# Sliding-window attention with sinks, then an MLP: one phase of matmul 1 and one mixed phase per batch, fp32 loads cast on the chip

## The chip, the cores and the metric

The kernel runs on one core of one Trainium2 chip. The time is the device time of one execution in microseconds (us). The kernel before takes 262.4 us (median of two executions, 262.15 to 262.66).

Engines: PE (TensorE, matmuls), PEld (its weight loads), DVE (VectorE), ACT (ScalarE), POOL (GpSimd), SP (the sync engine, which here only issues transfers).

## The reference

```python
# q, k, v: (4 batches, 8 heads, 768 tokens, 64); n_sink = 4, window = 128; all fp32
scores = (1 / sqrt(64)) * q @ k.T                      # per batch and head
keep = (key < n_sink) | ((0 <= query - key) & (query - key < window))
a = softmax(where(keep, scores, -1e9))
x = (a @ v), heads side by side                        # (3072 tokens, 512)
h = x @ w_in                                           # (512 -> 2048)   "matmul 1"
g = h * sigmoid(1.702 * h)
out = g @ w_out                                        # (2048 -> 512)   "matmul 2"
```

## The kernel before

A "unit" is a pair of heads of one batch (16 units). A loop over the units does attention for unit s, the AV product of unit s - 1, and, as filling between them, eight groups of matmul 1 and one or two tiles of matmul 2 of what is ready. All loads of q, k, v and the weights go through GpSimd's queue, which casts fp32 to fp16 on the way (by the page of this kernel 27.79 MB were read, and this queue, q0, wrote 13.64 MB). PSUM is the memory of the tiles that this kernel's matmuls write; DVE's copies below (0.41 to 0.42 us) take the transposes out of it.

```python
for hl in range(2):                        # loads of a unit: one head of q or k at a time, cast by the queue
    nc.gpsimd.dma_start(qn[:, :, hl], q[b, h0 + hl].rearrange("(i s) d -> s i d", s=P))
    nc.gpsimd.dma_start(kn[:, :, hl], k[b, h0 + hl].rearrange("(i s) d -> s i d", s=P))
...
for j in range(3):                         # t_chunk: transposes of q and k on PE, copied out of PSUM by DVE
    tp = misc_bank(f"tqk{su}_{j}", (P, 2, 2, P), FP16)
    ...
    nc.vector.tensor_copy(out=qkT[:, :, 2 * j * P : (2 * j + 2) * P], in_=tp)   # contiguous rows
...
for s in range(NU):                        # one unit of attention, matmul 1 and matmul 2 between its parts
    ...
    if s < 3:
        load_w_in(s + 1)
    elif s < 7:
        load_w_out(s - 3)
    fs = claim_f(s, 8)                     # matmul 1 groups that are ready
    m2 = claim_mm2(s, 2)                   # matmul 2 tiles that are ready
    s_chunk(s, 0); t_chunk(s + 1); av_chunk(s - 1, 0); s_chunk(s, 1); av_chunk(s - 1, 1)   # abridged
    ...                                    # f_chunk and mm2_chunk among xt_chunk(s - 1, ...)
    mask_chunk(s)
```

The softmax here doesn't subtract the row's maximum and nothing guards it: scores larger than these inputs give would overflow.

Of the kernel before, what the change touches and what calls it, by code (L numbers as in the profile page):

```python
# [9 lines left out]
FP32 = mybir.dt.float32  # L11
FP16 = mybir.dt.float16
AF = mybir.ActivationFunctionType
ALU = mybir.AluOpType
# [3 lines left out]
ACOLS = 1920  # L18
NQB = 6


def _acol(J: int, q0: int) -> int:
    if J == 0:
        return q0
    if J == 5:
        return 768 + (q0 - 640)
    return 896 + 256 * (J - 1) + (q0 - 128 * J)


def _build_mask(n_sink: int, window: int) -> np.ndarray:  # L30
    mask = np.zeros((P, ACOLS), dtype=np.float32)
    jj = np.arange(P)
    for J in range(6):
        if J == 0:
            qr = np.arange(0, 768)
        elif J == 5:
            qr = np.arange(640, 768)
        else:
            qr = np.arange(128 * J, 128 * J + 256)
        cols = np.array([_acol(J, int(t)) for t in qr])  # L40
        key = 128 * J + jj
        rel = qr[None, :] - key[:, None]
        keep = (key[:, None] < n_sink) | ((rel >= 0) & (rel < window))
        mask[:, cols] = keep.astype(np.float32)
    return mask.astype(np.float16)


SCORE_TILES = [
    ("s0", [(0, 0, 512)], 0),
    ("s1", [(0, 512, 256), (5, 640, 128)], _acol(0, 512)),  # L50
    ("s2", [(1, 128, 256), (2, 256, 256)], _acol(1, 128)),
    ("s3", [(3, 384, 256), (4, 512, 256)], _acol(3, 384)),
]
# [3 lines left out]
def kernel(  # L57
# [13 lines left out]
    assert (H, Dh) == (8, 64) and S == 768  # L71
# [6 lines left out]
    NU = Bsz * NHP  # L78
    NF = d_ff // P
    TT = 384  # L80
    NT4 = TT // P
# [3 lines left out]
    mask_d = nc.inline_tensor(_build_mask(n_sink, window), name="cmask")  # L85
# [3 lines left out]
    xtp = ctx.enter_context(tc.tile_pool(name="xtp", bufs=1))  # L89
    attn = ctx.enter_context(tc.tile_pool(name="attn", bufs=2))  # L90
    moep = ctx.enter_context(tc.tile_pool(name="moep", bufs=2))
    psp = ctx.enter_context(tc.tile_pool(name="psum", bufs=1, space=bass.MemoryType.PSUM))

    ident16 = const.tile([P, P], FP16, name="ident16")
    nc.sync.dma_start(ident16, ident16_d.ap())
    mask_all = const.tile([P, ACOLS], FP16, name="maskall")
    nc.sync.dma_start(mask_all, mask_d.ap())
    w_in16 = wpool.tile([P, 4, d_ff], FP16, name="w_in16")
    w_out16 = wpool.tile([P, NF, d_model], FP16, name="w_out16")
    xT = [xtp.tile([P, Bsz * S], FP16, name=f"xT{i}") for i in range(NHP)]  # L100

    def load_w_in(i: int):
        nc.gpsimd.dma_start(w_in16[:, i], moe_w_in[bass.ts(i, P), :])
# [7 lines left out]
    def sc_bank(name, shape=(P, 512), dt=FP32):  # L111
        return psp.tile(list(shape), dt, tag="sc", bufs=4, name=name)

    def ht_bank(name):
        return psp.tile([P, TT], FP32, tag="hT", bufs=2, name=name)

    def misc_bank(name, shape, dt):
        return psp.tile(list(shape), dt, tag="misc", bufs=2, name=name)

    U = [dict() for _ in range(NU)]  # L120

    def loads_qk(u: int):
        b, hp = divmod(u, NHP)
        h0 = 2 * hp
        su = f"{b}_{hp}"
        qn = attn.tile([P, NQB, 2, D], FP16, tag="qn", bufs=3, name=f"qn{su}")
        kn = attn.tile([P, NQB, 2, D], FP16, tag="kn", bufs=3, name=f"kn{su}")
        for hl in range(2):
            nc.gpsimd.dma_start(
                qn[:, :, hl], q[b, h0 + hl].rearrange("(i s) d -> s i d", s=P)  # L130
            )
            nc.gpsimd.dma_start(
                kn[:, :, hl], k[b, h0 + hl].rearrange("(i s) d -> s i d", s=P)
            )
        U[u].update(qn=qn, kn=kn)

    def loads_v(u: int):
        b, hp = divmod(u, NHP)
        h0 = 2 * hp
        su = f"{b}_{hp}"  # L140
        v65 = attn.tile([P, 2, NQB, D + 1], FP16, tag="v65", bufs=4, name=f"v65{su}")
        nc.vector.memset(v65, 1.0)
        nc.gpsimd.dma_start(  # L143
            v65[:, :, :, 0:D], v[b, h0 : h0 + 2].rearrange("h (i s) d -> s h i d", s=P)
        )
        U[u]["v65"] = v65

    def t_chunk(u: int):
        su = f"u{u}"
        qn, kn = U[u]["qn"], U[u]["kn"]  # L150
        qkT = attn.tile([P, 2, S], FP16, tag="qkT", bufs=2, name=f"qkT{su}")
        for j in range(3):
            tp = misc_bank(f"tqk{su}_{j}", (P, 2, 2, P), FP16)
            for i in range(2):
                I = 2 * j + i
                nc.tensor.transpose(tp[:, 0, i], qn[:, I], ident16)  # L156
                nc.tensor.transpose(tp[:, 1, i], kn[:, I], ident16)
            nc.vector.tensor_copy(out=qkT[:, :, 2 * j * P : (2 * j + 2) * P], in_=tp)
        U[u]["qkT"] = qkT

    def s_chunk(u: int, part: int):
        su = f"u{u}"
        qkT = U[u]["qkT"]
        if part == 0:
            U[u]["AT"] = attn.tile([P, 2, ACOLS], FP16, tag="AT", name=f"AT{su}")
        AT = U[u]["AT"]
        qT = [qkT[bass.ts(hl, D), 0] for hl in range(2)]
        kT = [qkT[bass.ts(hl, D), 1] for hl in range(2)]
        for nm, mms, c0 in SCORE_TILES[2 * part : 2 * part + 2]:
            st = [sc_bank(f"{nm}{su}_{hl}") for hl in range(2)]  # L170
            col = 0
            for J, q0, w in mms:
                for hl in range(2):
                    nc.tensor.matmul(  # L174
                        st[hl][:, col : col + w],
                        kT[hl][:, bass.ts(J, P)],
                        qT[hl][:, q0 : q0 + w],
                        start=True,
                        stop=True,
                    )  # L180
                col += w
            for hl in range(2):
                nc.scalar.activation(  # L183
                    out=AT[:, hl, c0 : c0 + col], in_=st[hl][:, 0:col],
                    func=AF.Exp, scale=scale,
                )

    def mask_chunk(u: int):
        AT = U[u]["AT"]
        for hl in range(2):  # L190
            nc.vector.tensor_tensor(
                out=AT[:, hl], in0=AT[:, hl], in1=mask_all, op=ALU.mult
            )

    def av_chunk(u: int, g: int):
        su = f"u{u}"
        AT, v65 = U[u]["AT"], U[u]["v65"]
        av = misc_bank(f"av{su}_{g}", (P, 3, 2, D + 1), FP32)
        xnat = attn.tile([P, 3, 2, D], FP16, tag="xnat", bufs=2, name=f"xn{su}_{g}")
        rcp = attn.tile([P, 3, 2], FP32, tag="rcp", bufs=2, name=f"rcp{su}_{g}")  # L200
        for i3 in range(3):
            I = 3 * g + i3
            Js = [J for J in (I - 1, I) if J >= 0] + ([0] if I >= 2 else [])
            for hl in range(2):
                for n, J in enumerate(Js):
                    c = _acol(J, P * I)
                    nc.tensor.matmul(
                        av[:, i3, hl],
                        AT[:, hl, c : c + P],
                        v65[:, hl, J],  # L210
                        start=(n == 0),
                        stop=(n == len(Js) - 1),
                    )
        nc.vector.reciprocal(out=rcp, in_=av[:, :, :, D])
        nc.vector.tensor_tensor(
            out=xnat, in0=av[:, :, :, 0:D],
            in1=rcp.to_broadcast((P, 3, 2, D)), op=ALU.mult,
        )
        U[u][f"xn{g}"] = xnat

    def xt_chunk(u: int, g: int):
        b, hp = divmod(u, NHP)
        su = f"u{u}"
        xnat = U[u][f"xn{g}"]
        xt = misc_bank(f"xt{su}_{g}", (P, 3, P), FP16)
        for i3 in range(3):
            nc.tensor.transpose(xt[:, i3], xnat[:, i3], ident16)
        c0 = b * S + 3 * g * P
        nc.vector.tensor_copy(out=xT[hp][:, c0 : c0 + 3 * P], in_=xt)

    gT = {}
    for bb in range(Bsz):
        for j in range(2):
            gT[bb, j] = moep.tile([P, NF, TT], FP16, tag="gT", name=f"gT{bb}_{j}")

    def f_chunk(b: int, j: int, F: int, nth: int):
        tok0 = b * S + j * TT
        su = f"{b}_{j}_{F}"
        hT = sc_bank(f"hT{su}", (P, TT)) if nth < 2 else ht_bank(f"hT{su}")
        for c in range(4):  # L240
            nc.tensor.matmul(  # L241
                hT, w_in16[:, c, bass.ts(F, P)], xT[c][:, tok0 : tok0 + TT],
                start=(c == 0), stop=(c == 3),
            )
        th = moep.tile([P, TT], FP16, tag="th", bufs=3, name=f"th{su}")
# [27 lines left out]
    def claim_f(s: int, cap: int):  # L273
        got = []
        while len(got) < cap and f_fifo and f_ready[f_fifo[0][0]] <= s:
# [4 lines left out]
            if f_done[bj] == NF:  # L280
                mm2_ready[bj] = s + 1
# [105 lines left out]
```

## Time and profile before

| stretch | PE busy | what holds |
|---|---|---|
| 0 to 50 us | 33.1 of 50 us | loads: the queues' share is at nine tenths |
| 50 to 256 us | 204.9 of 206 us | the matmul stream itself |

From the page of the kernel before: the span, and three rows of it in 40 equal slices of 6.5 us. A digit is the busy share of the slice in tenths; the last row is what the queues moved in GB/s.

```profile
span 260.1 us, 4792 instructions
PE   0749787999999999999999999999999999999993
DMA  9999999999959393595960140101021011111112
GB/s 137 139 175 182 176 173 175 179 174 136 92 73 117 20 115 20 106 63 73 61 79 35 8 65 22 59 3 40 4 79 44 0 42 40 43 40 40 40 43 81
```

The stretches of the same trace: start and end, length, then busy time of each engine (with instructions), the granted clock of PE, the queues' share (the times of all packets added up, so it can exceed 1; it is not the digit of the DMA row) and GB/s.

```profile
core 0: us, PE busy (x) PEld busy (x) DVE busy (x) ACT busy (x) POOL busy (x), PEclk, DMA share, GB/s
0.00:25.00 25.00, 13.08 (x107) 7.56 (x108) 11.62 (x21) 10.51 (x21) 20.91 (x30) 1.00 1.67 155
25.00:50.00 25.00, 20.04 (x265) 12.44 (x263) 22.98 (x51) 16.82 (x37) 19.70 (x25) 1.00 1.93 176
50.00:256.00 206.00, 204.90 (x1521) 111.43 (x1520) 123.95 (x250) 110.40 (x225) 33.70 (x40) 1.00 0.49 59
```

The period of the steady regime is read from ACT's line of time: start, duration, instruction. The same exp comes back two units later.

```profile
107.40 0.59 ACT L183 ACTIVATE ATu_1622<-s0u_0_1623 128x512 f16<-128x512 f32 x1
136.65 0.59 ACT L183 ACTIVATE ATu_2032<-s0u_0_2033 128x512 f16<-128x512 f32 x1
```

So a batch (four units) takes 2 x 29.25 = 58.5 us. Of that, 32 groups of matmul 1 take 0.65 us each (20.8 us) and six tiles of matmul 2 take 3.45 us each (20.7 us); the rest, 17 us, is attention, 4.25 us of PE time per unit.

### The profile page before, as it was taken

To read this page: it belongs to the slowest core of one execution; us is meant where nothing else is said; L and a number is where in the kernel's file an instruction comes from. 1 tells how busy PE (TensorE), PEld (TensorE's weight loads), DVE (VectorE), ACT (ScalarE), POOL (GpSimd) and SP (SyncE) were. 2 spreads that over 40 slices of the span, in tenths; PEclk is the share of its full clock that TensorE was granted. 3 is DMA by queue.
4 is the path that set the end of the run, shared out by engine and by line. 5 is a ranking of instruction groups with operands and counts; after the bars stand their busy time and mean duration, and the time that the engine had idled before them with its cause. 6 is when DMAs were issued, how large, how long until landed. Compare 5 with 4: busy or idle time off the path is not lost.

```text
span 260.1 us, 4792 instructions
## 1 busy us (share of the span) xinstructions
PE 238.2 (92%) x1888; PEld 131.4 (51%) x1888; DVE 158.6 (61%) x320; ACT 138.4 (53%) x282; POOL 74.3 (29%) x92
## 2 busy tenths in 40 slices
PE   0749787999999999999999999999999999999993
PEld 0415444565646464555546464555545555555541
DVE  4337989898958685495918684493915833543300
ACT  1257666868438483757538483757533633644311
POOL 8977788773535151133310100000000000000000
PEclk9999999999999999999999999999999999999999
DMA  9999999999959393595960140101021011111112
GB/s 137 139 175 182 176 173 175 179 174 136 92 73 117 20 115 20 106 63 73 61 79 35 8 65 22 59 3 40 4 79 44 0 42 40 43 40 40 40 43 81
DMA packets 81607, 20.76 MB, mean 80 GB/s; under 512 B 75697, under 2 KB 78001, under 8 KB 81585
## 3 DMA queue, kind: packets, MB, share of 16 engines
q0 software_dynamic: 77696, 13.64, 66.1%
q1 hardware_dynamic: 3888, 6.82, 7.1%
q8 instruction: 15, 0.25, 0.4%
q14 instruction: 8, 0.06, 0.1%
HBM read 27.79 MB, written 6.29 MB: 131 GB/s over the span
## 4 chain that ended last, share of the span: by engine, by line
PE 82%; ACT 5%; DVE 4%; POOL 3%; DMA 3%; issue 1%; ACTq 0%; POOLq 0%
DMA qn_2_126<-in_q_dram 3%; PE o_1_2_3359 L257 1%; PE o_1_1_3339 L257 1%; PE o_1_0_3319 L257 1%; PE o_0_2_3267 L257 1%; PE o_0_1_3215 L257 1%; PE o_0_0_3163 L257 1%; PE o_1_2_3079 L257 1%; PE o_1_1_3027 L257 1%; PE o_1_0_2975 L257 1%; PE o_0_2_2809 L257 1%; PE o_0_1_2771 L257 1%; PE o_1_2_2584 L257 1%; PE o_1_1_2395 L257 1%; PE o_0_1_1985 L257 1%; PE o_0_0_1965 L257 1%
## 5 line engine op out<-in xcount | busy, mean ns | idle before, releaser
L241 PEld LDWEIGHTS <-w_in_77 128*128 128x128 f16 x512 | 47.8, 98 | 31.4 <-issue 1.1
L257 PEld LDWEIGHTS <-gT_1_90 128*128 128x128 f16 x48 | 4.7, 98 | 5.5
L257 PEld LDWEIGHTS <-gT_0_89 128*128 128x128 f16 x48 | 4.7, 98 | 5.3
L257 PEld LDWEIGHTS <-gT_0_87 128*128 128x128 f16 x48 | 4.7, 98 | 5.3
L257 PEld LDWEIGHTS <-gT_1_88 128*128 128x128 f16 x48 | 4.7, 98 | 5.3
L257 PEld LDWEIGHTS <-gT_1_84 128*128 128x128 f16 x48 | 4.7, 98 | 5.2
L257 PEld LDWEIGHTS <-gT_0_85 128*128 128x128 f16 x48 | 4.7, 98 | 5.2
L257 PEld LDWEIGHTS <-gT_1_86 128*128 128x128 f16 x48 | 4.7, 98 | 5.2
L156 PE MATMUL tqku_0_108<-ident_73,qn_0_91 128*128 128x128 f16 x2 | 0.6, 288 | 7.1 <-DMA qn_0_91<-in_q_dram 7.1
L257 PEld LDWEIGHTS <-gT_0_83 128*128 128x128 f16 x48 | 4.7, 98 | 4.8
L143 POOL DMA_DIRECT2D v_3_2433<-in_v_dram x1 | 1.0, 1007 | 15.3 <-issue 15.3
L183 ACT ACTIVATE ATu_136<-s0u_0_137 128x512 f16<-128x512 f32 x1 | 0.6, 597 | 7.9 <-PE s0u_1_138 L174 7.9
L156 PEld LDWEIGHTS <-qn_0_91 128*128 128x128 f16 x6 | 0.7, 125 | 7.1 <-issue 7.1
L247 DVE SCALAR_TENSOR_TENSOR gT_0_87<-th_0_6_2420,hT_0_6_2415 128x384 f16<-128x384 f16 x1 | 0.6, 553 | 5.9 <-ACT th_0_6_2420 L246 5.9
L257 PE MATMUL o_0_0_1145<-w_out_78,gT_0_83 128*128 128x512 f16 x16 | 4.1, 379 | 0.0
L247 DVE SCALAR_TENSOR_TENSOR gT_1_88<-th_1_6_2796,hT_1_6_2791 128x384 f16<-128x384 f16 x1 | 0.6, 554 | 5.7 <-ACT th_1_6_2796 L246 5.7
L247 DVE SCALAR_TENSOR_TENSOR gT_0_85<-th_0_6_1600,hT_0_6_1595 128x384 f16<-128x384 f16 x1 | 0.6, 553 | 5.3 <-ACT th_0_6_1600 L246 5.3
L247 DVE SCALAR_TENSOR_TENSOR gT_1_86<-th_1_6_2010,hT_1_6_2005 128x384 f16<-128x384 f16 x1 | 0.6, 553 | 5.3 <-ACT th_1_6_2010 L246 5.3
L257 PE MATMUL o_0_2_1360<-w_out_78,gT_0_83 128*128 128x512 f16 x16 | 3.8, 379 | 0.0
L257 PE MATMUL o_0_0_1965<-w_out_78,gT_0_85 128*128 128x512 f16 x16 | 3.8, 379 | 0.0
L257 PE MATMUL o_1_2_2584<-w_out_78,gT_1_86 128*128 128x512 f16 x16 | 3.8, 379 | 0.0
L257 PE MATMUL o_1_0_2375<-w_out_78,gT_1_86 128*128 128x512 f16 x16 | 3.8, 379 | 0.0
(1546 smaller groups left out, 810.9 us busy)
## 6 DMA issues: line engine op xcount, KB each, us to landing
w_in_77<-in_moe_w_in_dram POOLq DMA_DIRECT2D x4, 512.0 KB, 8.6
w_out_78<-in_moe_w_out_dram POOLq DMA_DIRECT2D x4, 512.0 KB, 8.8
maskall<-cmask SPq DMA_DIRECT2D x1, 480.0 KB, 3.9
out_dram<-osb_0_0_1146 SPq DMA_DIRECT2D x1, 256.0 KB, 2.1
out_dram<-osb_0_1_1166 SPq DMA_DIRECT2D x1, 256.0 KB, 3.6
out_dram<-osb_0_2_1361 SPq DMA_DIRECT2D x1, 256.0 KB, 3.6
out_dram<-osb_1_0_1556 SPq DMA_DIRECT2D x1, 256.0 KB, 3.7
out_dram<-osb_1_1_1576 SPq DMA_DIRECT2D x1, 256.0 KB, 2.3
```

The source lines that it names most:

```text
L143: nc.gpsimd.dma_start(v65[:, :, :, 0:D], v[b, h0 : h0 + 2].rearrange("h (i s) d -> s h i d", s=P))
L156: nc.tensor.transpose(tp[:, 0, i], qn[:, I], ident16)
L183: nc.scalar.activation(out=AT[:, hl, c0 : c0 + col], in_=st[hl][:, 0:col], func=AF.Exp, scale=scale,)
L241: nc.tensor.matmul(hT, w_in16[:, c, bass.ts(F, P)], xT[c][:, tok0 : tok0 + TT], start=(c == 0), stop=(c == 3),)
L247: nc.vector.scalar_tensor_tensor(out=gT[b, j][:, F], in0=th, scalar=1.0, in1=hT, op0=ALU.add, op1=ALU.mult)
L257: nc.tensor.matmul(ops, gT[b, j][:, F, bass.ts(t4, P)], w_out16[:, F], start=(F == 0), stop=(F == NF - 1),)
```

## The change

Its intent: fewer, larger instructions and a simpler stream for PE. Per batch there is a phase of matmul 1 alone, then a phase in which matmul 2 is mixed with the attention of the next batch. Attention goes by half-units (one pair of heads, 384 of the 768 tokens). q, k and v are loaded as fp32 by the sync queue, q and k with three successive tokens on one partition (768 bytes in a piece), and cast on DVE, GpSimd and ACT. The weights wait behind batch 0's loads, and batch 1's loads behind the weights. Part of the mask becomes GpSimd selects.

The diff, cut to its core (the matmul code, the mask and the pools are left out; cuts are marked):

```diff
-            nc.gpsimd.dma_start(
-                qn[:, :, hl], q[b, h0 + hl].rearrange("(i s) d -> s i d", s=P)
-            )
+            nc.sync.dma_start(                                   # loads(m): two units, 384 tokens, fp32
+                qk32[:, t].rearrange("p h i d -> p h (i d)"),
+                s[b, hs, t0 : t0 + SLAB].rearrange("h (p i) d -> p h (i d)", i=NB),
+            )
+            nc.sync.dma_start(v32[:, i], v[b, hs, ti : ti + P].rearrange("h s d -> s h d"))
 ...
+                eng = nc.vector if early and t == 0 else nc.gpsimd     # casts(m); early: batch 0
+                eng.tensor_copy(
+                    qk16[:, j, t].rearrange("p i h d -> p h i d"),
+                    L[m]["qk32"][:, t, 2 * j : 2 * j + 2],
+                )
+        (nc.scalar.copy if early else nc.gpsimd.tensor_copy)(v65[:, :, :, 0:D], L[m]["v32"])
 ...
-            nc.vector.tensor_copy(out=qkT[:, :, 2 * j * P : (2 * j + 2) * P], in_=tp)
+        nc.vector.tensor_copy(                                   # puts the token triples in order again
+            out=qkT.rearrange("d t i s -> d t (i s)").rearrange("d t (s i) -> d t i s", i=NB), in_=tp
+        )
 ...
+            nc.gpsimd.affine_select(...)                         # part of the mask, per half-unit
 ...
+    casts(0)
+    for kk in range(2 * NHP):                                    # batch 0: attention alone
+        attention(kk, lambda i: None)
+        if kk == 1:
+            after(w_in16[0:1, :, 0:1], L[3]["qk32"][...])        # GpSimd copy: a gate
+            for i in range(4):
+                load_w_in(i)
+            for i in range(4):
+                load_w_out(i)
+            for m in range(4, 8):
+                loads(m, w_out16[0:1, 11, 0:1] if m == 4 else None)   # the same, behind w_out
+    av_chunk(2 * NHP - 1)
+    xt_chunk(2 * NHP - 1)
+
+    for b in range(Bsz):
+        for F in range(NF):
+            f_chunk(b, F)                                        # matmul 1, alone
+        ...
+            for r in range(2 * NHP):
+                attention(k0 + r, fill)                          # fill: pieces of matmul 2
```

Within `attention(kk)` the order is: scores of half-unit kk, transposes of q and k of kk + 1, AV of kk - 1, mask of kk, transposes of the output of kk - 1.

## The prediction

> **What bounds the kernel now.** The stretches of the span show two regimes. From about 50 us to 256 us PE is busy 99% of the time at a granted clock of 1.00: there it is the matmul stream, back to back. The chain of waits gives its pieces: 0.65 us per 4-matmul group of matmul 1 (128 groups, 83 us) and 3.45 us per 16-matmul tile of matmul 2 (24 tiles, 83 us). A steady period of two attention units takes 29.24 us (one exp to the same exp two units later) and holds 16 groups and 3 tiles, 20.75 us; so a unit of attention costs 4.25 us of PE time, of which about 0.45 us is waiting for the exps. The first 50 us are the other regime: PE about 70% busy, DMA row at nine tenths, 170 to 180 GB/s written, which for fp32-to-fp16 casting loads is some 350 GB/s read. The start is bound by loading; matmul 1 flows only from about 46 us.
>
> **What the change does.** Matmul 1 and 2 stay (166 us). Score exps go from 8 to 4 per unit, the mask leaves VectorE in part, tanh and gate cover 768 columns. None of this is on the PE-bound path beyond the 0.45 us exp wait. I estimate a unit at 3.4 us (transposes 0.68, scores 0.8, AV 0.95, output transposes 0.34, the rest about 0.1 us for each change between 64-row and 128-row matmuls, as in the trace). For 12 units that saves about 10 us.
>
> Against it, batch 0 no longer overlaps anything. By the instruction order PE meets matmul 1 of batch 0 in earnest only after its last attention piece, at T0. GpSimd's order decides T0: the copy that gates batch 1's loads waits for the third piece of w_out, and behind it on the same engine stand the masks of half-units 2 to 7 and casts that wait for batch 1's loads. At 300 to 350 GB/s, 4.7 MB of q, k, v and 7.3 MB of weights need until about 36 to 41 us (estimate)[...]: T0 about 50 to 54 us. After T0 come 80 us of matmul 1, 83 of matmul 2, 41 of attention, 4 of tail and the 2 us between span and time: 210.
>
> A second risk is GpSimd in the mixed phase: four selects per second-half half-unit. [...] No trace here shows a select. This may cost 0 to 10 us.
>
> **Prediction.** 259 us; 8 times in 10 between 247 and 271. Faster by over 2%: 0.42; within 2%: 0.38; slower: 0.20.
>
> **What would show it.** Right: PE mostly idle before 45 us, GpSimd waiting for w_out at 25 to 38 us, PE at 99% from about 52 us, matmul-1 phases of 20.8 us per batch with no waits for VectorE, mixed phases of about 34 us. Wrong at T0: matmul 1 of batch 0 flowing before 45 us (then about 250 us) or after 58 us. Wrong in the mixed phase: waits of PE for GpSimd's selects, over 1 us per half-unit.
>
> **What would make it wrong.** Hardware-queue loads of 768 B and 256 B much faster or slower than the casting ones; selects or casts on GpSimd twice my estimate; output stores queued behind loads on the sync queue, holding the two output buffers; weights landing faster when alone.

The loads' 36 to 41 us and the term for the work behind them came to 50 to 54 us, with a middle of 52. With the 210 us after T0 the sum is 262, where the prediction says 259. An estimate of GpSimd's selects was no term of its own in this sum, and the 0 to 10 us of the second risk, like "twice my estimate", rested on it.

Some other figures of the prediction, with what they come from in the trace of the kernel before: the 300 to 350 GB/s are about twice the 155 and 176 GB/s written in the first two stretches. In a unit, transposes follow each other on PE at 0.057 us (107.40 to 107.80 us), so 12 make 0.68 us. The 0.1 us for a change: a 64-row score matmul of 128 columns starts at 107.25 us and the first 128-row transpose 0.15 us later, where transposes of as many columns take 0.057. The 0.45 us for the exps: two score tiles start at 108.05 and 108.54 us, 0.06 and 0.05 us after the ends of two exps on ACT, which is 0.19 and 0.27 us later than PE's steps just before (0.057 and 0.11 us from start to start) would put them; the first of the two holds a change as well.

## More of the kernel before

The copies of the transposed q and k on DVE, which will matter, are three of 512 elements per unit, written contiguously. Two of them from DVE's line of time:

```profile
108.01 0.42 DVE L158 COPY qkTu_1637<-tqku_0_1638 128x512 f16<-128x512 f16 x1
108.34 0.41 DVE L158 COPY qkTu_1637<-tqku_1_1644 128x512 f16<-128x512 f16 x1
```

## The result and the profile after

The changed kernel takes 286.63 us (median of two executions, 286.34 and 286.93), against 262.4. The ratio is 1.091, interval 1.085 to 1.097: slower. A ratio here is the mean time of one kernel's runs over that of the other's in the same rounds, so it is not quite the ratio of the medians. Executions over 1.5% slower than the fastest of the same kernel are left out of the means.

The page of the changed kernel, the same rows (slices of 7.1 us):

```profile
span 284.5 us, 5065 instructions
PE   0223334887999999999998899999988999999994
DMA  7999999999921315850031401100010111000212
GB/s 190 208 207 255 189 204 225 273 255 260 244 66 39 104 49 184 213 137 2 0 113 43 144 37 60 52 3 0 2 39 37 39 39 74 2 0 0 74 76 74
```

The nines of PE begin after the tenth slice, at about 71 us, and the eights among them (149 to 163 and 206 to 220 us) lie in mixed phases. So there are two losses, one at the start and one that comes back every batch.

**The start.** What waited between 8 and 66 us (engine, instruction, what it waited for, total, times, longest):

```profile
engine line waited for: us in total, times, longest us
POOL qk_4_237 L82 <- DMA w_out_77<-in_moe_w_out_dram: 13.5, 1, 13.5
ACT L142 <- DMA v_0_91<-in_v_dram: 10.7, 1, 10.7
...
PE av_343 L249 <- POOL AT_275 L221: 7.6, 1, 7.6
PE sA_183 L167 <- ACT AT_158 L176: 7.1, 1, 7.1
...
ACT v_1_141 L142 <- DMA v_1_98<-in_v_dram: 6.3, 1, 6.3
```

PE's two long waits after its first input had come are for other engines, and those were standing still themselves. On ACT, the first exp of the kernel stands behind the casts of three loads of v, although its scores were finished at 15.4 us. ACT's line of time (start, duration, instruction, in brackets the idle time before it and what ended it):

```profile
19.19 0.83 ACT L142 CAST v_1_141<-v_1_98 128x768 f16<-128x768 f32 x1 [6.33 <-DMA v_1_98<-in_v_dram]
23.30 0.83 ACT L142 CAST v_2_267<-v_2_105 128x768 f16<-128x768 f32 x1 [3.27 <-DMA v_2_105<-in_v_dram]
24.03 1.02 ACT L176 ACTIVATE AT_158<-sA_159 128x1024 f16<-128x1024 f32 x1
```

On GpSimd the gate copy of batch 1's loads waits for the third piece of w_out, and the masks of half-units of batch 0 wait behind it:

```profile
31.07 0.54 POOL L138 CAST qk_2_269<-qk_2_104 128x384 f16<-128x384 f32 x1
45.14 0.18 POOL L82 CAST qk_4_237<-w_out_77 1x2 f32<-1x2 f16 x1 [13.53 <-DMA w_out_77<-in_moe_w_out_dram]
...
45.84 0.40 POOL L221 TENSOR_SCALAR_AFFINE_SELECT AT_275<-AT_275 128x256 f16<-128x256 f16 x1
```

The last output of batch 0's attention is copied at 64.03 us. Call this moment T0; the prediction had 50 to 54 us. (It counts from the start of the span, as do all moments here.)

**The mixed phases.** The interval from the sixth output tile of one batch to the sixth of the next is 59.01 us (121.17 to 180.18 us, ACT's evictions). Before, a batch took 58.5 us: in its steady regime the changed kernel is no faster at all. Less 20.8 us for matmul 1 alone, a mixed phase takes 38.2 us, and less 20.7 us for matmul 2, attention takes 17.5 us, 4.4 us a unit; the prediction had 3.4. The stretch of one mixed phase, with the columns as above:

```profile
core 0: us, PE busy (x) PEld busy (x) DVE busy (x) ACT busy (x) POOL busy (x), PEclk, DMA share, GB/s
142.00:180.00 38.00, 35.15 (x384) 18.78 (x381) 22.46 (x38) 16.56 (x22) 20.06 (x42) 1.00 0.23 77
```

PE is idle there for 2.85 us, and no other engine is near full. DVE's line of time in it shows why:

```profile
161.01 1.45 DVE L153 COPY qkT_1958<-tqk_1959 128x768 f16<-128x768 f16 x1 [1.24 <-PE tqk_1959 L152]
162.31 0.16 DVE L252 RECIPROCAL rcp_1969<-av_1967 128x6 f32<-128x6 f32 x1
162.52 0.56 DVE L253 TENSOR_TENSOR xn_1968<-av_1967,rcp_1969 128x384 f16<-128x384 f32 x1
```

And PE's, just after:

```profile
163.13 0.34 PE L263 MATMUL xt_1992<-ident_86,xn_1968 128*128 128x128 f16 x3 [0.28 <-DVE xn_1968 L253]
163.41 0.39 PE L167 MATMUL sA_2005<-qkT_1958 64*128 64x256 f16 x4
```

The copy of the transposes now writes its 768 elements three apart, and takes 1.45 us. The normalisation of the half-unit before stands behind it on DVE, PE's output transposes wait for that, and the next scores stand behind those. In each half-unit this chain must fit within 4.2 to 4.4 us beside PE's own work.

The prediction lacked a figure for such a copy. Taken over the whole instruction, this one takes 1450 ns for 768 elements, 1.89 ns an element. The copy before, contiguous, took 420 ns for 512, 0.82 ns an element. So in these traces the scattered copy takes 2.3 times as long an element; why is not shown. Experiment 2 takes the scatter from the write to the read, and there it is 0.95 us, 1.24 ns an element.

**Two theories.** A: work stands behind instructions that wait for late loads, as on GpSimd (13.53 us) and ACT (6.33 and 3.27 us) above (start), and the scattered copy in DVE's chain delays PE (start and mixed phases). B, the rivals: the fp32 loads on the sync queue are slower than the casting ones (start), and GpSimd's selects and casts hold the mixed phases. Each has its own experiment below.

### The profile page after: what moved, and what is told of

Same layout as the page of the kernel before. It is cut to its first block, busy times and chain, and to the rows that moved or that the text cites. A ratio compares the mean times of both kernels' runs of the same rounds, so it can differ in the third digit from the quotient of the medians.

```text
span 284.5 us, 5065 instructions
## 1 busy us (share of the span) xinstructions
PE 234.4 (82%) x2048; PEld 131.9 (46%) x2048; DVE 154.6 (54%) x238; ACT 126.5 (44%) x186; POOL 80.9 (28%) x176
## 3 DMA queue, kind: packets, MB, share of 16 engines
q0 software_dynamic: 5808, 4.25, 9.9%
## 5 line engine op out<-in xcount | busy, mean ns | idle before, releaser
L280 PEld LDWEIGHTS <-w_in_76 128*128 128x128 f16 x512 | 50.0, 98 | 37.2 <-DMA w_in_76<-in_moe_w_in_dram 4.0
L299 PEld LDWEIGHTS <-gT_85 128*128 128x128 f16 x96 | 9.4, 98 | 11.2
L299 PEld LDWEIGHTS <-gT_82 128*128 128x128 f16 x96 | 8.0, 97 | 7.4 <-issue 0.2
L299 PEld LDWEIGHTS <-gT_84 128*128 128x128 f16 x96 | 8.0, 97 | 7.2 <-issue 0.2
L299 PEld LDWEIGHTS <-gT_83 128*128 128x128 f16 x96 | 8.0, 97 | 7.2 <-issue 0.2
L138 POOL CAST qk_14_2614<-qk_14_2076 128x384 f16<-128x384 f32 x4 | 1.9, 507 | 23.5 <-PE tqk_2535 L152 23.5
L138 POOL CAST qk_10_1797<-qk_10_1252 128x384 f16<-128x384 f32 x4 | 1.9, 507 | 22.7 <-PE tqk_1711 L152 22.7
L249 PE MATMUL av_343<-v_1_141,AT_275 128*128 128x65 f16 x10 | 0.9, 240 | 8.1 <-POOL AT_275 L221 7.6
L167 PE MATMUL sA_183<-qkT_171 64*128 64x256 f16 x4 | 0.6, 398 | 7.1 <-ACT AT_158 L176 7.1
L152 PEld LDWEIGHTS <-qk_0_135 128*128 128x128 f16 x12 | 1.0, 124 | 9.8 <-DVE qk_0_135 L138 8.8
L221 POOL TENSOR_SCALAR_AFFINE_SELECT AT_869<-AT_869 128x256 f16<-128x256 f16 x1 | 0.4, 407 | 17.5 <-ACT AT_869 L194 17.5
L280 PE MATMUL hT_2_0_656<-xT_78,w_in_76 128*128 128x384 f16 x4 | 1.9, 485 | 3.9 <-DMA w_in_76<-in_moe_w_in_dram 3.9
L176 ACT ACTIVATE AT_375<-sA_376 128x1024 f16<-128x1024 f32 x1 | 1.0, 1023 | 8.6 <-PE sA_376 L167 8.6
L249 PEld LDWEIGHTS <-AT_275 128*128 128x128 f16 x12 | 0.8, 128 | 8.6 <-POOL AT_275 L221 7.8
L167 PEld LDWEIGHTS <-qkT_171 64*128 64x128 f16 (+1 forms) x18 | 0.9, 109 | 7.9 <-issue 7.8
L299 PE MATMUL o_0_1706<-w_out_77,gT_83 128*128 128x512 f16 x16 | 4.5, 381 | 0.0
L299 PE MATMUL o_0_2530<-w_out_77,gT_84 128*128 128x512 f16 x16 | 4.5, 381 | 0.0
L299 PE MATMUL o_3_1177<-w_out_77,gT_82 128*128 128x512 f16 x16 | 4.5, 380 | 0.0
L299 PE MATMUL o_3_2001<-w_out_77,gT_83 128*128 128x512 f16 x16 | 4.5, 380 | 0.0
L299 PE MATMUL o_3_2811<-w_out_77,gT_84 128*128 128x512 f16 x16 | 4.5, 380 | 0.0
```

What stands on the lines that cost most here:

```text
L138: eng.tensor_copy(qk16[:, j, t].rearrange("p i h d -> p h i d"), L[m]["qk32"][:, t, 2 * j : 2 * j + 2],)
L152: nc.tensor.transpose(tp[:, t, i], qk[:, t, i], ident16)
L167: nc.tensor.matmul(dst.rearrange("p (t s) -> p t s", s=P), key[hd[h]], qkT[hd[h], 0, i0 : i0 + ni], start=True, stop=True,)
L176: nc.scalar.activation(out=AT[:, 0:8].rearrange("p (h a) s -> p h (a s)", h=2), in_=A, func=AF.Exp, scale=scale)
L221: nc.gpsimd.affine_select(out=ap, in_=ap, pattern=[[0, ap.shape[1]], [sgn, P]], compare_op=ALU.is_ge if sgn > 0 else ALU.is_gt, fill=0.0, ...
L249: nc.tensor.matmul(av[:, i, h], lhsT, rhs, start=(m == 0), stop=(m == len(terms) - 1))
```

## The experiments

T0 is the start of the copy of batch 0's last attention output, "first tile" the start of the first output tile's eviction, "period" the interval between the sixth output tiles of two successive batches, all from each run's trace. The ratio is against the kernel before in the same rounds.

| kernel | T0 | first tile | period | time, us (median) | ratio |
|---|---|---|---|---|---|
| changed | 64.03 | 90.23 | 59.01 | 286.63 | 1.091 |
| without the gate | 63.80 | 90.01 | 59.00 | 284.38 | 1.083 |
| contiguous copy | 62.74 | 88.48 | 56.03 | 276.51 | 1.052 |
| without selects (wrong result) | 63.14 | 89.33 | 58.94 | 285.28 | 1.087 |
| batch 0 in program order | 47.84 | 81.86 | 59.01 | 278.99 | 1.062 |
| + weights early | 47.55 | 76.45 | 59.01 | 272.86 | 1.038 |
| + contiguous copy | 47.74 | 76.37 | 56.03 | 265.58 | 1.010 |
| + transposes ahead | 44.20 | 75.97 | 56.02 | 264.96 | 1.008 |
| + GpSimd in order in batch 1 | 44.10 | 72.86 | 56.03 | 262.29 | 1.002 |
| + weights a little later | 43.43 | 71.83 | 56.02 | 261.31 | 0.997 |
| + pieces of matmul 1 in batch 0 | 44.44 | 67.96 | 56.02 | 257.08 | 0.979 |

### 1. Without the gate (label e1_nogate)

```diff
-                loads(m, w_out16[0:1, 11, 0:1] if m == 4 else None)
+                loads(m)
```

> The gate of batch 1's loads (the copies from the third piece of w_out, on GpSimd) is gone; nothing else in the source changes. Queue theory: GpSimd's 13.5 us wait at 31 to 45 us disappears, the selects of half-units 2 and 3 run some 10 us earlier, the last piece of batch 0's attention moves from 63.9 us to 50 to 56 us, time 273 to 280. Rival, loading theory: batch 0 is held by the bytes that have to land, and ungated loads only compete with the weights; the last piece moves by less than 4 us, time 283 to 287.

Measured: 284.38 us (two executions, 282.61 and 286.15), ratio 1.083, interval 1.069 to 1.096: no difference from the changed kernel that is clear of the noise. The 13.5 us wait is gone, and T0 did not move (63.80 us). These are the figures that the rival, the loading theory, named; the trace decides what held T0. The reason is in GpSimd's line of time of this run:

```profile
56.35 0.83 POOL L142 CAST v<-v 128x768 f16<-128x768 f32 x1 [1.33 <-DMA v<-in_v_dram]
...
58.91 0.82 POOL L142 CAST v<-v 128x768 f16<-128x768 f32 x1 [1.65 <-DMA v<-in_v_dram]
59.69 0.77 POOL L221 TENSOR_SCALAR_AFFINE_SELECT AT<-AT 128x256 f16<-128x256 f16 x2
```

and in PE's:

```profile
60.51 0.29 PE L249 MATMUL av<-v,AT 128*128 128x65 f16 x2 [3.12 <-POOL AT L221]
```

Half-units 2 to 6 came earlier (the third output at 43.80 us in place of 48.25), but now the last masks stand behind casts of batch 1's loads on the same engine, and before them PE waits 5.9 us for w_in. The expectation of theory A failed for the gate alone: taking the longest wait away let the next one in the same queue take its place. Whether the theory is right needs all of them away at once (experiment 5).

### 2. The copy of the transposes made contiguous (label e2_copy)

```diff
-            out=qkT.rearrange("d t i s -> d t (i s)").rearrange("d t (s i) -> d t i s", i=NB), in_=tp
+            out=qkT.rearrange("d t i s -> d t (i s)").rearrange("d t (s i) -> d t s i", i=NB),
+            in_=tp.rearrange("d t i s -> d t s i"),
```

The same elements go to the same places in another order: now the write is contiguous and the read of PSUM hops.

> The copy of the transposed q and k out of PSUM writes contiguous fp16 and reads with a stride of 128 elements, in place of writing with a stride of 3. Theory: the strided write makes this copy slow (1.45 us for 768 elements against 0.42 for 512 before) and it stands in the chain copy, reciprocal, normalise, transpose of the mixed phase; the copy falls to 0.6 to 0.9 us, each mixed phase of 38 us to 35 to 36 us, time down by 6 to 9 us to about 278 to 281. Rival: GpSimd's selects or PE itself set the mixed phase; the copy gets shorter but the time falls by under 2 us.

Measured: 276.51 us (four executions, 276.16 to 276.61), ratio 1.052. That is 10 us less than the changed kernel, from one line, and a little more than the 6 to 9 us expected. In the trace the copy takes 0.95 us:

```profile
155.47 0.96 DVE L153 COPY qkT<-tqk 128x768 f16<-128x768 f16 x1 [1.24 <-PE tqk L152]
156.34 0.18 DVE L253 RECIPROCAL rcp<-av 128x6 f32<-128x6 f32 x1
156.56 0.56 DVE L254 TENSOR_TENSOR xn<-av,rcp 128x384 f16<-128x384 f32 x1
```

and the stretch of one mixed phase of this run (columns as above) is 35.9 us long, with PE idle for only 0.5 us of it:

```profile
138.00:173.90 35.90, 35.37 (x390) 19.39 (x389) 19.55 (x38) 17.16 (x23) 19.85 (x42) 1.00 0.25 82
```

The period falls by 2.98 us, twice; the stretch from T0 to the sixth tile of batch 0, which holds the first mixed phase, falls by 2.5 us, and T0 by 1.3: together the whole difference of the two traces (9.7 us). The copies took 0.49 us less each, 0.49 x 8 = 3.9 us per batch, so three quarters of DVE's saved time was on PE's path. GpSimd did the same work in this stretch as before (19.85 us busy against 20.06), and PE hardly waits: neither its selects nor its casts hold the mixed phase.

### 3. The selects left out (label e12_nosel, wrong)

```diff
-        for ap, sgn in sel:
+        for ap, sgn in sel if kk < 2 * NHP else []:
```

> The changed kernel as it came, without the GpSimd selects of batches 1 to 3 (wrong on purpose: the parts of the band that they clear stay). It takes away the risk that the prediction named: 24 units-halves times about 1.9 us of selects. If the selects are on the critical path of the mixed phases: 10 us or more less, 277 us or below. If the mixed phases are held by the chain through DVE's scattered copy: 284 to 287 us, unchanged.

Measured: 285.28 us (four executions), period 58.94 us against 59.01, relative error 0.38 as meant. The selects of the mixed phases are worth 0.07 us a batch. (Most of the 1.35 us in all lie at the start, where T0 came 0.9 us earlier.) With what experiment 2 showed of the casts, the rival of the mixed phases falls.

### 4. The loads by themselves (label e4_dma, output zeros)

A kernel with only loads, between barriers: one batch's q, k and v as the changed kernel loads them, another's as the kernel before does, another's as fp32 in 256-byte rows on the sync queue, then w_in.

> A kernel of loads alone (its output is zeros, wrong on purpose): between barriers, one batch's q, k and v (4.7 MB of fp32) as the changed kernel loads them, one as the kernel before loads them, one as fp32 in 256-byte rows, and then w_in. Loading theory: fp32 on the sync queue is slower than the casting queue even alone, 20 to 24 us against 14 to 16 us, and the 256-byte rows slower than the triples, over 25 us; w_in (4.2 MB read) takes about 12 us. Rival: alone the ways are equally fast (within 2 us), and the slow start of the changed kernel is contention and issue.

Measured in a single execution, from the first issue to the last landing: changed way 19.2 us, way before 20.9 us, 256-byte rows 24.1 us, w_in 13.1 us. Alone, the loads of the changed kernel are no slower than those before; the rival of the start, that they are slower in themselves, falls. (What they meet when the weights load beside them is the matter of experiments 6 and 7.) The 256-byte rows cost a quarter more than the mixture of 768-byte and 256-byte pieces. But the 256-byte way also made 36 issues where the changed way made 20, and this run does not separate the size of the pieces from the number of issues.

### 5. Batch 0 in program order (label e5_order)

Each of PE, ACT, DVE and GpSimd is made to run batch 0 in the order in which the program states it, with everything later behind; the casts of the next loads come after the scores of the half-unit before; w_in is issued after half-unit 5 and w_out after the batch; the gate is a 4-byte copy on the loads' own queue.

```diff
-        if kk % 2 == 0 and kk + 2 < NK and kk % (2 * NHP) < 6:
+        first = kk < 2 * NHP
+        if not first and kk % 2 == 0 and kk + 2 < NK and kk % (2 * NHP) < 6:
             casts(kk // 2 + 1)
 ...
         s_chunk(kk)
+        if first and kk % 2 == 1 and kk < 6:
+            casts(kk // 2 + 1)
 ...
-            after(qk32[0:1, :, 0, 0, 0:1], src.to_broadcast((1, 2, 1)))
-            after(v32[0:1, :, 0, 0:1], src.to_broadcast((1, NB, 1)))
+            for dst in (qk32[0:1, 0, 0, 0, 0:1], qk32[0:1, 1, 0, 0, 0:1]):
+                nc.sync.dma_start(dst, src)
+            for i in range(NB):
+                nc.sync.dma_start(v32[0:1, i, 0, 0:1], src)
 ...
+        for ins in list(nc.cur_bb.bb.instructions)[start:]:      # pinned(start)
+            if ins.engine in last:
+                tc.add_manual_dep(ins, last[ins.engine].name, info, reason="pinned")
+            last[ins.engine] = ins
```

> Batch 0's attention keeps program order on PE, ScalarE, VectorE and GpSimd, everything later is issued behind it; each cast follows the scores that don't need it; the weights are issued after half-unit 5, and the gate of batch 1's loads is a small copy on the sync queue. The same work and the same loads. Queue theory: each engine no longer stands behind a load that comes later than the work behind it (ScalarE until 24.0 us for v casts, PE until 35.0 us for w_in, GpSimd until 45.1 us for w_out); the last piece of batch 0's attention comes at 29 to 36 us and the time is 250 to 259. Loading theory: it comes at 45 us or later, time 268 or more.

Measured: 278.99 us, ratio 1.062. T0 fell by 16.2 us, to 47.84, which the gate alone had not done at all; but the queue theory had it at 29 to 36 us and the time at 250 to 259. Both figures lie where the rival, the loading theory, had put them (45 us or later, 268 or more), so this run alone does not decide between the two; experiment 6 does. Two things were missed. First, batch 0 without load waits is a chain of about 4.2 us per half-unit, the same copy, normalisation and output transposes as in the mixed phases. DVE's line of time:

```profile
21.43 1.43 DVE L155 COPY qkT<-tqk 128x768 f16<-128x768 f16 x1 [1.50 <-PE tqk L154]
22.71 0.17 DVE L254 RECIPROCAL rcp<-av 128x6 f32<-128x6 f32 x1
22.92 0.56 DVE L255 TENSOR_TENSOR xn<-av,rcp 128x384 f16<-128x384 f32 x1
```

and PE's, which waits for it in each half-unit:

```profile
19.38 0.50 PE L265 MATMUL xt<-ident,xn 128*128 128x128 f16 x3 [1.49 <-DVE xn L255]
23.53 0.50 PE L265 MATMUL xt<-ident,xn 128*128 128x128 f16 x3 [1.49 <-DVE xn L255]
```

In these lines stands something more, which the experiments did not look into. Three output transposes take 0.50 us here and 0.34 us in the mixed phase shown above. From start to start, PE's own work of a half-unit of this kind is about 2.7 us here (19.38 to 22.04 us) and about 1.4 us in that mixed phase, though the clock column shows 1.00 in both stretches. So of the 4.2 us, 1.5 are PE's wait for DVE, and the rest is PE itself at about half its later pace. The changed kernel has the same: 0.50 us until 51.65 us, 0.34 from 55.30 on. The kernel before has 0.34 from 24.57 us on. Why is not shown, and no run separates it from the DVE chain.

Second, the weights and batch 1's loads came late for it: the first output tile came 34.0 us after T0, against 26.2 in the changed kernel, with one wait of GpSimd for batch 1's q of 16.5 us.

### 6, 7, 8. Early weights, the contiguous copy, transposes ahead (labels e6_early, e7_early_copy, e8_deep)

Each adds one edit to the one before (e8_deep, besides the transposes, issues batch 0's casts one half-unit earlier, behind the mask). The gate of batch 1's loads stays as in experiment 5.

```diff
# e6_early
+        if 1 <= kk <= 4:
+            for i in range(2):
+                (load_w_in if kk < 3 else load_w_out)(2 * (kk - 1) % 4 + i)
# e7_early_copy: the line of e2_copy
# e8_deep, in batch 0 only
         if lo:
             t_chunk(kk)
+        if first and (kk + 1) % (2 * NHP):
+            t_chunk(kk + 1)                 # before the scores of kk
         s_chunk(kk)
-        if first and kk % 2 == 1 and kk < 6:
-            casts(kk // 2 + 1)
+        if first and kk > 1:
+            xt_chunk(kk - 2)                # output transposes two half-units behind
 ...
         mask_chunk(kk)
+        if first and kk % 2 == 0 and kk < 6:    # the casts, one half-unit earlier than in e7
+            casts(kk // 2 + 1)
```

> The pinned order of the run before (batch 0 in program order on every engine), with the weights issued early: w_in after half-units 1 and 2, w_out after half-units 3 and 4, without a gate. The copy of the transposes stays scattered. Theory A (batch 0 alone is a latency chain of about 4.2 us per half-unit, and what was lost after it was late weights and late batch-1 loads): the last batch-0 transposes stay at 47 to 49 us, the first output tile is evicted 26 to 28 us later in place of 34 us, time 269 to 273 us. Rival B (the loads set the pace of batch 0): loads of weights now share the bandwidth with batch 0's loads, so the last batch-0 transposes come later, 52 us or more, and the time stays at 276 us or more.

Measured: 272.86 us, T0 47.55, first tile 28.9 us after T0. As theory A had it, except that the last figure is 1 us longer. The weights' traffic did not delay batch 0 (T0 was 47.84 us without it), so the loads did not set its pace here: rival B falls for this order.

> As the run before in this job, plus the copy of the transposes with its writes contiguous and its PSUM reads strided (one line). Theory A: 8 half-units of batch 0 lose about 0.5 us each and the three mixed phases about 3 us each, so the last batch-0 transposes come at 43 to 45 us, the mixed phases take about 35 us and the time is 256 to 260 us, which is at or a little below the kernel before (262.4). Rival (PE work alone sets the mixed phase and the gain of the copy in the earlier run was luck of the order): 267 or more.

Measured: 265.58 us, between the two expectations. The period fell to 56.03 us, as expected, and by the same 2.98 us as in experiment 2: the two edits add up. But T0 stayed at 47.74. One instruction ate the gain of the start, again a cast in front of what did not need it. ACT's line of time in this run:

```profile
37.51 0.83 ACT L144 CAST v<-v 128x768 f16<-128x768 f32 x1 [5.11 <-DMA v<-in_v_dram]
```

Batch 0's fourth load of v lands 5.1 us after ACT is ready for it, while w_out is on its way (its pieces are issued from 24.96 to 30.70 us and land 14.5 us after issue in the median). In e6_early ACT came to the same cast 2.6 us later, and the load landed 2.9 us earlier (34.5 us against 37.4), so it did not wait. Once the chain is shorter, a load holds batch 0 again.

> As the run before in this job, and in batch 0 alone the transposes of q and k go one half-unit ahead of the scores, and those of the attention output come two half-units behind, so that PE waits for neither copy nor normalisation. Theory A (latency chain): about 3.5 us per half-unit, last batch-0 transposes at 39 to 42 us, 252 to 257 us, over 2% faster than the kernel before. Rival (batch 0 is bound by the work of an engine or by loads): no change from the run before, within 1 us.

Measured: 264.96 us, the figure of the rival; but T0 fell to 44.20, 3.5 us, the direction of theory A with half of its size. What was gained at T0 was lost before the first output tile (75.97 against 76.37). PE's line of time in this run:

```profile
74.20 0.23 PE L252 MATMUL av<-v,AT 128*128 128x65 f16 x1 [2.60 <-POOL AT L224]
```

and GpSimd's, where the masks of batch 1's first half-units stand behind casts that wait for loads:

```profile
70.69 0.83 POOL L144 CAST v<-v 128x768 f16<-128x768 f32 x1 [3.38 <-DMA v<-in_v_dram]
71.46 2.32 POOL L140 CAST qk<-qk 128x384 f16<-128x384 f32 x4
73.74 0.77 POOL L224 TENSOR_SCALAR_AFFINE_SELECT AT<-AT 128x256 f16<-128x256 f16 x2
```

### 9. Casts on the queue, as before, within the changed kernel (label e3_swload)

The loads of the changed kernel go to GpSimd's queue, head by head, and are cast on the way; no fp32 tiles and no casts on the engines.

```diff
-            nc.sync.dma_start(
-                qk32[:, t].rearrange("p h i d -> p h (i d)"),
-                s[b, hs, t0 : t0 + SLAB].rearrange("h (p i) d -> p h (i d)", i=NB),
-            )
+                for hl in range(2):
+                    nc.gpsimd.dma_start(
+                        qk16[:, j, t, :, hl],
+                        s[b, 2 * hp + 2 * j + hl, t0 : t0 + SLAB].rearrange("(p i) d -> p i d", i=NB),
+                    )
```

> The changed kernel with one part undone: q, k and v are cast to fp16 by GpSimd's queue on their way in, as in the kernel before, without fp32 tiles and without casts on the engines; token triples, phases and weights stay. If the fp32 loads with casts on the chip are what lost the time: 265 to 275 us. If they are worth nothing either way (the schedule and the scattered copy lost it): 282 to 292 us, since issuing 44 loads of batch 0 occupies GpSimd for about 37 us, ahead of the masks of its first half-units.

Measured: 331.71 us, ratio 1.262, far outside both expectations. GpSimd issues the loads at 0.77 us each, 44 for batch 0, until 35 us, and its first mask comes at 37.6 us; batch 0's last output is copied at 101 us. In the first 25 us the queues moved 70 GB/s. Later the gate waits 15.3 us for w_out on GpSimd, and the next masks come only at 74.30 us, behind batch 1's issues. So undoing the cast in this way gains nothing within this schedule. It is not a clean test of the cast: it also makes 44 issues where the kernel before makes 20 per batch, and puts GpSimd's masks behind the issues. That casting on the chip lost no time is therefore not shown by this run.

### 10. GpSimd in order in batch 1, then the weights later (labels e9_poolq, e10_later)

```diff
# e9_poolq: casts of the next loads after the masks of the running half-unit, GpSimd pinned there
+        second = 2 * NHP <= kk < 4 * NHP
+        if second and kk % 2 == 0 and kk % (2 * NHP) < 6:
+            casts(kk // 2 + 1)              # at the end of the half-unit
# e10_later
-        if 1 <= kk <= 4:
+        if kk in (2, 3, 5, 6):
```

> The last run (batch 0 pinned, transposes ahead, early weights, contiguous copy; 264.96 us) with one more queue put in order: in batch 1's half-units GpSimd keeps program order too, and its casts of the next loads come after the masks of the running half-unit, so no mask stands behind a cast that waits for its load. If the in-order queue behind late loads is what cost the 5 us between the last batch-0 transposes and the first output tile (31.8 us against 27 in the later batches): first output tile 4 to 5 us earlier, 259.5 to 262 us. If those 5 us are the total loading (batch 0, weights and batch 1 share one bandwidth up to about 66 us): no gain, 264 to 266 us.

Measured: 262.29 us, first tile 3.1 us earlier with T0 unchanged: the queue behind late loads was what cost it, though for 3 us rather than 5 (the time is just above the range given for it).

> As the run before in this job, with the weights issued later: w_in after half-units 2 and 3, w_out after 5 and 6, so that batch 0's own loads meet less traffic. If the loads' sharing of bandwidth held batch 0's last half-units in the run before (waits for casts of its third and fourth load): last batch-0 transposes at 40 to 42 us in place of 44.2, and 256 to 259 us. If batch 0 is a chain that loads do not hold: no change of that time, and the later weights cost 0 to 3 us.

Measured: 261.31 us, ratio 0.997 (0.995 to 1.000), T0 43.43. The gain lies between the two expectations; issuing the weights later is worth about 0.7 us at T0, and their traffic is not what mainly holds batch 0 now. What does was not tested; in this trace PE waits three times for 2.1 to 2.2 us for casts of q on DVE, which stand behind DVE's masks there. (The clock column has 0.50 here from 25 to 35 us, and 1.00 in e9_poolq from 20 to 35 us; but three transposes take 0.50 us in both, at 32.16 and 32.42 us, so the column does not tell the two runs apart.)

### 11. Matmul 1 where PE waits in batch 0 (label e11_fill)

```diff
+        if kk >= 6:
+            f_half(0, kk - 6, 0)            # matmul 1, tanh and gate for the first 384 tokens alone
+    f_half(0, 2, 0)
     xt_chunk(2 * NHP - 2)
+    f_half(0, 3, 0)
     av_chunk(2 * NHP - 1)
+    f_half(0, 4, 0)
+    f_half(0, 5, 0)
     xt_chunk(2 * NHP - 1)
```

> The best version so far (261.31 us), and in the last two half-units of batch 0 and its tail, six pieces of matmul 1 for the first half of the tokens (whose attention is done by then) stand where PE waits. If PE's idle time there (about 3.5 us between the fourth attention output and the start of matmul 1) is what is left on the critical path: 258 to 260 us. If the pieces delay the attention chain as much as they save later: 261 to 263 us.

Measured: 257.08 us (four executions, 256.66 to 257.38), correct, ratio 0.979, interval 0.976 to 0.983. It is 1 us better than the expectation. T0 is 1 us later and the first tile 3.9 us earlier. PE does the pieces where it stood still, as its line of time in this run shows:

```profile
36.60 0.81 PE L297 MATMUL hT<-xT,w_in 128*128 128x384 f16 x4
...
39.02 1.46 PE L297 MATMUL hT<-xT,w_in 128*128 128x384 f16 x8
```

This version beats both kernels: 257.08 us against 262.24 for the kernel before in the same rounds and 286.63 for the changed one. Against the kernel before the gain is clear of the noise; whether it is over 2%, the interval leaves open.

## Why the prediction was right or wrong

It was wrong: 259 us with 247 to 271, where 286.63 came. The missing 27.6 us can be counted out. 12 us lie in T0 (64.0 us, the middle of the prediction's 50 to 54 being 52). About 11.5 us lie in attention after T0 (three batches at 17.5 us against 41 in all). Some 3 us are the prediction's own: its terms add up to 52 + 210 = 262, and it said 259. The last 1 us is within the reading of the phases' ends.

- **"What bounds the kernel now"** was right for the steady regime. The matmul groups of 0.65 and 3.45 us returned unchanged. That the start of the kernel before is bound by loading was not tested.
- **"I estimate a unit at 3.4 us" is the first step that failed.** It added up PE's own instructions and took the rest for hidden. The unit took 4.4 us, no less than the 4.25 of before. Of the 1.0 us, 0.75 (2.98 us per period over four units) is shown by e2_copy to come from the scattered copy in DVE's chain, and went away with one line. What stays is 3.63 us (56.03 less 20.8 and 20.7, over four units) against the 3.4: PE's own work, mis-sized by 0.1 to 0.2 us, and up to 0.13 us of waiting (with the contiguous copy PE is busy for 35.4 of 35.9 us).
- **"T0 about 50 to 54 us" is the second step that failed.** The mechanism, masks behind a gate that waits for w_out, was there, with a wait of 13.5 us, but the third piece of w_out landed at 45.1 us in place of 36 to 41, and the chain of work behind it took 18.9 us, where the forecast (50 to 54 less 36 to 41) left it 13 to 14, the author's estimate. It was also not the only thing: e1_nogate took it away and T0 stayed. ACT's exp behind casts of v, PE behind w_in, and masks behind casts of batch 1 each take over. Keeping program order with casts and weights moved (e5_order) took off 16.2 us; what then remained was about 4.2 us per half-unit, of which 1.5 us are the wait for the DVE chain and the rest is PE's own work at about half its later pace. The prediction had no term for that pace; why it was so stays open. e5_order changes several things together, so how the 16.2 us divide among them stays open too.
- **"A second risk is GpSimd in the mixed phase"**, 0 to 10 us, did not come true. A select of 512 elements took 0.63 us and one of 256 took 0.41, the four of a half-unit, two of each, took 1.94 us, and without the selects the period changed by 0.07 us. (The author's own estimate of a select was not worked out from a trace.)
- **"What would show it"** worked: T0 after 58 us was named as the sign of an error at the start. A wait of PE for selects was the sign for the mixed phase, and it was the wrong engine to watch there.
- **"Hardware-queue loads of 768 B and 256 B much faster or slower than the casting ones"** did not happen. Alone, the ways took 19.2 and 20.9 us (one execution).

The idea of the change was sound in its parts. With the contiguous copy a batch takes 56.0 us against 58.5 before in the steady regime; it is the start that ate this, and the start could be mended by the order of the work (in the last step with six groups of matmul 1 split in halves).

## What to carry to other kernels

In these traces an instruction that waited for a load held the work behind it on its engine (13.5 us on GpSimd, 6.3 us on ACT), so place casts, gates and other load-dependent work after the work that is ready, and take all such waits away before judging one of them: the removal of the longest alone gained nothing at T0. When a layout change makes a copy scatter its output, measure that copy (here 768 elements took 1.45 us scattered and 0.95 us with a contiguous write) and follow the chain through its engine; DVE held PE here while it was busy for 59% of the mixed phase (22.46 of 38 us). The start-up without filler, once it waited for no load, was a chain of about 4.2 us per half-unit, in which PE and DVE took turns; measure such a chain in a trace of a start, since PE's own work of a half-unit took about 2.7 us there and about 1.4 us in the mixed phase shown above.
